# Two-layer linear attention and gated feed-forward on one core: key weights loaded as groups of full rows, first key tiles computed part by part

## The chip, the cores and the metric

One Trainium2 chip, one of its cores. The metric is the device time of one execution in microseconds (us). TensorE is called PE, VectorE DVE, ScalarE ACT, GpSimd POOL, as in the profile.

## The reference, cut to what matters

```python
def _A_ref(x, wqkv, wo):                      # linear attention, 32 heads of 32
    qkv = (x @ wqkv) ...                      # q, k, v
    phi = lambda t: jnp.where(t > 0, t + 1, jnp.exp(t)) + 1e-6
    pq, pk = phi(q), phi(k)
    kv = einsum("bhsd,bhse->bhde", pk, v); z = einsum("bhsd->bhd", pk)
    o = einsum("bhqd,bhde->bhqe", pq, kv) / (einsum("bhqd,bhd->bhq", pq, z)[..., None] + 1e-6)
    return o @ wo                             # heads merged again
def _B_ref(x, w_gate, w_up, w_down):
    return ((x @ w_gate) * (x @ w_up)) @ w_down

x = A_x                                       # 2048 tokens x 1024, bfloat16
x = x + _A_ref(_layernorm(x), A_wqkv, A_wo)
x = x + _B_ref(_layernorm(x), B_w_gate, B_w_up, B_w_down)
x = x + _A_ref(_layernorm(x), A_wqkv, A_wo)
x = x + _B_ref(_layernorm(x), B_w_gate, B_w_up, B_w_down)
```

## The kernel before

Every operation is recorded in program order for its engine; semaphore waits are derived from what it reads and writes. So the order of the calls below is the order on each engine. The change and the argument touch only the opening of the first attention layer. A token tile is 128 tokens; there are 16.

The layer norm of a tile: statistics on DVE, reciprocal root on POOL, normalisation on DVE.

```python
def ln_a(i):
    for h in range(2):   P.add("dve", bn_stats of half h of x_res[:, i])
    P.add("dve", bn_aggr)
    P.add("pool", variance + eps)
    P.add("pool", pow -0.5)                 # ln_rstd
# tiles 5, 7, 9, 11, 13: statistics by two ACT passes (ln_s1 copy with sum, ln_s2 square with sum)
# and the same POOL steps behind ln_s2; ln_b2: normalise on DVE, (x - mean) * rstd
```

A tile is then transposed, by PE and a copy out of PSUM for the first four, by DMA from tile 4 on:

```python
if self.to == "A0" and n == 0:              # tile 0 in two halves, ACT and DVE
    for hf, b in enumerate((B_TP, B_KQ[3])):
        P.add("pe", 4 transposes);  P.add(("act", "dve")[hf], copy of that half)
    return
P.add("pe", 8 transposes);  P.add("act", copy of the whole tile)
```

The opening, with `proj(kind, i, h)` the 8 matmuls of one column half of a tile and `ev` its feature map phi (exp and relu on ACT, minimum and sum on DVE):

```python
lnp.start(0); lnp.b_one(); lnp.step_t(1)    # tile 0: statistics, normalise, transpose
...three warm-up matmuls...
lnp.start(1); lnp.b_one()
# inside the first projections: transposes of tile 1 in (k,0,h=1), of tile 2 in (k,1,h=1)
mids = {("k", 0, 0): lambda: None, ("k", 0, 1): lambda: lnp.step_t(1), ("k", 1, 1): lambda: lnp.step_t(1)}
lead = [[start(2)], [b_one], [start(3)], [b_one], [], [step_t(1)], [start(4)], [b_one, start(5)]]
for kind, i in seq:                         # k0 k1 k2 q0 k3 q1 k4 ...
    for h in range(2):
        ev = proj(kind, tok[i], h, mids.pop(...)); ev()
        if lead: ...the next entry, and for k2 one weight difference (128x2048) on DVE...
        elif kind == "k": lnstep(i, h)      # h=0: start(next tile), then b_one() of the tile before
```

The loads, all on one queue:

```python
dma(x tile 0, columns 0-511); dma(x tile 0, columns 512-1023)
for hf in range(2):
    dma(k weights, rows of 4 of the 8 row blocks, columns 0-511)
xload(1); load_w("k", 1)                    # k columns 512-1023, all 8 row blocks
xload(2); load_w("q", 0); xload(3); load_w("q", 1); xload(4); xload(5)
```

## Time and profile before

| | |
|---|---|
| time, three runs at first | 1436.43 us median (1435.66 to 1438.34) |
| span of the profile | 1433.9 us |
| PE busy | 1420.6 us, 99% |
| first useful PE work | 6.46 us |
| PE restart for the second half of the key weights | 11.23 us |
| start of key tile 2 | 18.14 us |

A line of the timeline gives start, length, engine, source line, operation, output and input, shape, count, and in brackets the idle time ahead of it with what ended it. A line merges several instructions and lengths are modelled, so two lines can overlap (12.11 + 0.61 against 12.55 in the kernel before); starts are what to compare. The prediction below shows the opening's lines and reads them.

### The profile page before, as it was taken

To read this page: it belongs to the slowest core of one execution; us is meant where nothing else is said; L and a number is where in the kernel's file an instruction comes from. 1 tells how busy PE (TensorE), PEld (TensorE's weight loads), DVE (VectorE), ACT (ScalarE), POOL (GpSimd) and SP (SyncE) were. 2 spreads that over 40 slices of the span, in tenths; PEclk is the share of its full clock that TensorE was granted. 3 is DMA by queue.
4 is the path that set the end of the run, shared out by engine and by line. 5 is a ranking of instruction groups with operands and counts; after the bars stand their busy time and mean duration, and the time that the engine had idled before them with its cause. 6 is when DMAs were issued, how large, how long until landed. Compare 5 with 4: busy or idle time off the path is not lost.

```text
span 1433.9 us, 21771 instructions
## 1 busy us (share of the span) xinstructions
PE 1420.6 (99%) x8107; PEld 786.8 (55%) x8167; DVE 1209.5 (84%) x2370; ACT 688.2 (48%) x1408; POOL 149.9 (10%) x181
## 2 busy tenths in 40 slices
PE   9999999999999999999999999999999999999999
PEld 4444444555546566664544444446766475666547
DVE  6897878999988799988679978778888887888888
ACT  5882355444410266652157813667776004767400
POOL 2203621000010000002000045310000100000000
PEclk9999999999999999999999999999999999999999
DMA  7868978997786777768993266767775976777653
GB/s 227 203 144 234 219 173 199 300 303 266 255 266 211 235 256 255 244 235 300 232 286 96 89 171 165 182 181 254 262 243 194 288 256 226 261 258 259 205 192 120
DMA packets 272586, 320.73 MB, mean 224 GB/s; under 512 B 164064, under 2 KB 215008, under 8 KB 272480
## 3 DMA queue, kind: packets, MB, share of 16 engines
q1 hardware_dynamic: 272480, 319.34, 73.1%
q8 instruction: 64, 1.05, 0.3%
q14 instruction: 42, 0.34, 0.1%
HBM read 236.45 MB, written 73.40 MB: 216 GB/s over the span
## 4 chain that ended last, share of the span: by engine, by line
PE 84%; DVE 8%; ACT 2%; DMA 2%; issue 2%; POOL 1%; SPq 1%; POOLq 0%; DVEq 0%; ACTq 0%
PE ps L1385 28%; PE ps L1466 17%; PE ps L1802 14%; PE ps L1201 8%; PE ps L960 6%; PE ps L1720 5%; PE ps L1303 4%; DVE arena L798 3%; PE ps L928 2%; DMA arena<-arena 1%; DVE arena L453 1%; DVE arena L801 1%; DMA arena<-in_A_wqkv_dram 1%; ACT arena L658 1%; SPq L426 1%
## 5 line engine op out<-in xcount | busy, mean ns | idle before, releaser
L798 DVE TENSOR_TENSOR arena<-arena 128x512 f16<-128x512 f16 (+9 forms) x1019 | 498.8, 517 | 60.1 <-ACT arena L1470 34.2
L1385 PE MATMUL ps<-arena 128*128 128x512 f16 x1888 | 457.0, 379 | 1.0 <-DVE arena L801 0.9
L801 DVE SCALAR_TENSOR_TENSOR arena<-ps,arena 128x512 f16<-128x512 f32 (+3 forms) x545 | 353.8, 663 | 68.5 <-PE ps L1802 28.4
L1466 PE MATMUL ps<-arena 128*128 128x256 f16 x2184 | 287.5, 273 | 1.0 <-DVE ps L1479 1.0
L1385 PEld LDWEIGHTS ps<-arena 128*128 128x128 f16 (+1 forms) x1888 | 182.9, 98 | 163.4 <-ACT ps L1414 3.8
L1466 PEld LDWEIGHTS ps<-arena 128*128 128x128 f16 (+1 forms) x2184 | 212.2, 98 | 91.5 <-ACT arena L1470 6.9
L1802 PE MATMUL ps<-arena 128*128 128x512 bf16 (+1 forms) x1102 | 242.6, 379 | 0.9
L1802 PEld LDWEIGHTS ps<-arena 128*128 128x128 f16 x1120 | 109.5, 98 | 130.4 <-DVE arena L798 0.4
L1390 ACT ACTIVATE arena<-ps 128x512 f32<-128x512 f32 x224 | 133.8, 597 | 76.4 <-PE ps L1385 61.6
L1470 ACT ACTIVATE arena<-ps 128x256 f32<-128x256 f32 x351 | 125.1, 384 | 26.9 <-PE ps L1466 22.0
L960 PE MATMUL ps<-arena 128*128 128x512 f16 (+1 forms) x606 | 134.1, 379 | 1.0 <-ACT arena L967 0.4
L1201 PE MATMUL ps<-arena 128*128 128x512 bf16 x498 | 114.7, 379 | 0.7
L1303 PE MATMUL ps<-arena 128*128 128x512 bf16 x502 | 110.3, 379 | 0.5
L456 POOL TENSOR_SCALAR arena<-arena 128x1 f32<-128x1 f32 x59 | 20.8, 353 | 806.8 <-DVE arena L455 806.8
L1476 ACT COPY ps<-ps 128x256 f32<-128x256 f32 x182 | 66.3, 364 | 74.6 <-DVE arena L801 28.3
L960 PEld LDWEIGHTS ps<-arena 128*128 128x128 f16 x616 | 59.5, 98 | 74.7 <-ACT arena L967 5.8
L1414 ACT COPY ps<-ps 128x512 f32<-128x512 f32 x112 | 65.4, 584 | 64.3 <-PE ps L1385 52.1
L1062 POOL TENSOR_TENSOR arena<-arena 128x1024 f16<-128x1024 f32 x32 | 78.2, 2445 | 154.6 <-DVE arena L1060 146.3
L1720 PE MATMUL ps<-arena 128*128 128x256 f16 (+1 forms) x784 | 86.8, 273 | 0.7 <-DVE arena L801 0.5
L453 DVE BATCH_NORM_STATS2 arena<-arena 128x6 f32<-128x512 bf16 x118 | 81.3, 689 | 5.4 <-DMA arena<-in_A_x_dram 3.3
L1479 DVE TENSOR_TENSOR ps<-ps,arena 128x256 f32<-128x256 f32 x182 | 76.6, 427 | 10.5 <-PE ps L1466 9.5
L1303 PEld LDWEIGHTS ps<-arena 128*128 128x128 f16 x512 | 50.1, 98 | 60.4
(70 smaller groups left out, 939.8 us busy)
## 6 DMA issues: line engine op xcount, KB each, us to landing
arena<-w_scratch SPq DMA_DIRECT2D x84, 896.0 KB, 4.6
arena<-t_scratch SPq DMA_DIRECT2D x32, 896.0 KB, 6.1
arena<-in_B_w_down_dram SPq DMA_DIRECT2D x24, 896.0 KB, 5.7
arena<-sp_scratch SPq DMA_DIRECT2D x26, 768.0 KB, 4.2
w_scratch<-arena SPq DMA_DIRECT2D x28, 512.0 KB, 6.3
arena<-w_scratch SPq DMA_DIRECT2D x28, 384.0 KB, 4.8
x_scratch<-arena SPq DMA_DIRECT2D x40, 256.0 KB, 7.7
arena<-x_scratch SPq DMA_DIRECT2D x40, 256.0 KB, 5.6
```

Of the source, the lines that this page charges most:

```text
L453: P.add("dve", (lambda h: lambda e: e.bn_stats(st[j][:, 6 * h:6 * h + 6], x_res[:, i, (D // 2) * h:(D // 2) * (h + 1)]))(h), rd=r_x(i, (D ...
L798: P.add("dve", lambda e: e.tensor_tensor(out=out, in0=a, in1=b, op=op), rd=rd, wr=wr, prd=prd)
L801: P.add("dve", lambda e: e.scalar_tensor_tensor(out=out, in0=a, scalar=sc, in1=b, op0=ALU.mult, op1=op1), rd=rd, wr=wr, prd=prd)
L960: P.add("pe", lambda e: [e.matmul(psb(bank), a[0][:, k, :], b[0][:, k, :], start=(q in (1, 5) and k == 0), stop=(k == 3), skip_group_check ...
L1201: return [e.matmul(psb(bank), xrt[t][:, jj * 128:(jj + 1) * 128], pk[:, h, t, :], start=(t == tok[0]), stop=(t == tok[NST - 1])) for t in ts]
L1303: return [e.matmul(psb(bank), xnT[:, g, i * 128:(i + 1) * 128], wp[:, g, dh * 512:(dh + 1) * 512], start=(dh == 0 and g == 0), stop=(g == ...
L1385: P.add("pe", lambda e: [e.matmul(psb(bank), w[:, k, :], x[:, k, :], start=(start and k == 0), stop=(k == 3), skip_group_check=True) for k ...
L1390: P.add("act", lambda e: e.activation(t, psb(bank), AF.Copy, scale=SG), prd=[bank], wr=r)
L1466: P.add("pe", lambda e: [e.matmul(psb(bank)[:, 256 * half:256 * half + 256], w[:, k, :], xx[:, k, :], start=(start and k == 0), stop=(k == ...
L1470: P.add("act", lambda e: e.activation(d, src, AF.Copy, scale=sc), prd=[xk], wr=rd_)
L1720: P.add("pe", lambda e: [e.matmul(psb(bank)[:, 256 * half:256 * half + 256], a[:, k, 128 * r:128 * r + 128], b[:, k, :], start=(start and ...
L1802: P.add("pe", lambda e: [e.matmul(psb(bank), hv[:, 7 * hf + k, t * 128:(t + 1) * 128], w[:, k, :], start=(q in "15" and hf == 0 and k == 0 ...
```

## The change

Its intent is to have PE begin the keys as rows of the weights land, instead of waiting for whole column halves, and to get tile 1's transposes and the copies out of the way. The diff, cut to its core:

```diff
-        def ln_a(i):
+        def ln_a(i, mid=None):              # mid() is recorded between the two statistics halves
...
-                if self.to == "A0" and n == 0:
-                    for hf, b in enumerate((B_TP, B_KQ[3])):
+                if self.to == "A0" and n < 3:
+                    for hf, b in enumerate((B_TP, B_KVT[0])):
+                        dv = hf and n < 2   # tiles 0, 1: ACT and DVE; tile 2: both halves on ACT
...
-                lnp.step_t(1)
+                lnp.start(1, lambda: lnp.step_t(1))
                 ...three warm-up matmuls...
-                lnp.start(1)
...
+            if first:
+                for k in (0, 2, 4):
+                    p0(range(k, k + 2))     # column half 0 of key tile 0, two row blocks
+                    p1_(range(k, k + 2))    # column half 1
+                lnp.step_t(1)               # transposes of tile 1
+                p0(range(6, 8))
+                p1_(range(6, 8))
+                lnp.start(2)
+                lnp.b_one()
+                e0_()
+                e1_()
+                pt1(range(KT))              # key tile 1
+                pt1b(range(0, 4))
+                lnp.step_t(1)               # transposes of tile 2
+                pt1b(range(4, KT))
+                lnp.start(3)
+                et1()
+                lnp.b_one()
+                et1b()
+                seq = seq[NHOLD:]
...
-        for hf in range(2):
-            dma(wk[:, 4 * hf:4 * hf + 4, 0:512], ...)
         xload(1)
-        load_w("k", 1)
-        xload(2)
-        load_w("q", 0)
+        for k, key in ((0, KW["k"][0]), (2, KKB), (4, KW["k"][1]), (6, KKC)):
+            if k == 6:
+                xload(2)
+            w_rows("k", k, 2, key)          # two row blocks, all 1024 columns
+        w_rows("q", 0, 4, KW["q"][0])
         xload(3)
-        load_w("q", 1)
+        w_rows("q", 4, 4, KW["q"][1])
```

More of the change, by code (lines that the diff above doesn't have):

```diff
@@ L294, in build_kernel @@
     KKB = dkey("k0b")
+    KKC = dkey("k0c")
     KXS = [dkey("xs%d" % i) for i in range(NST)]
@@ L454, in ln_a @@
                       rd=r_x(i, (D // 2) * h, (D // 2) * (h + 1)), wr=R(O_ST[j] + 24 * h, 24))
+                if mid and h == 0:
+                    mid()
             P.add("dve", lambda e: e.bn_aggr(mv[j][:, 0:2], st[j]), rd=R(O_ST[j], 48), wr=R(O_MV[j], 8))
@@ L514, in dst, with start @@
                 return vh(o, D), R(o, D * 2)
-            def start(self, i):
+            def start(self, i, mid=None):
                 assert i == self.n
@@ L521, in start @@
                 else:
-                    j = ln_a(self.order[i])
+                    j = ln_a(self.order[i], mid)
                 self.n += 1
@@ L579, in transpose @@
                               rd=r + R(O_IDENT, 256), pwr=[b])
-                        P.add(("act", "dve")[hf], (lambda hf, tq_: lambda e: (e.tensor_copy if hf else e.copy)(xnT[:, 4 * hf:4 * hf + 4, i * 128:(i + 1) * 128], tq_))(hf, tq_),
+                        P.add(("act", "dve")[dv], (lambda hf, tq_, dv=dv: lambda e: (e.tensor_copy if dv else e.copy)(xnT[:, 4 * hf:4 * hf + 4, i * 128:(i + 1) * 128], tq_))(hf, tq_),
                               prd=[b], wr=_seg(O_XT + 4 * hf * S * 2, 4, S * 2, i * 256, (i + 1) * 256))
@@ L925, in proj, with ev, part @@
                 kq_i[0] += 1
+                def ev():
+                    phi_evac(bank, *dst_of(kind, i, h))
+                    if kind == "k" and tok.index(i) % 2 and h:
+                        z_pair(tok.index(i) // 2)
+                def part(ks):
+                    P.add("pe", lambda e: [e.matmul(psb(bank), xnT[:, k, i * 128:(i + 1) * 128], t[:, k, h * 512:(h + 1) * 512],
+                                                    start=(k == 0), stop=(k == KT - 1)) for k in ks],
+                          rd=r_xT(i * 128, (i + 1) * 128)[ks[0]:ks[-1] + 1] + r_w(base, h * 512, (h + 1) * 512)[ks[0]:ks[-1] + 1], pwr=[bank])
+                if mid == "parts":
+                    return part, ev
                 for ks in ((range(0, 4), range(4, 8)) if mid else (range(KT),)):
@@ L933, in proj @@
                         mid = None
-                def ev():
-                    phi_evac(bank, *dst_of(kind, i, h))
-                    if kind == "k" and tok.index(i) % 2 and h:
-                        z_pair(tok.index(i) // 2)
                 return ev
@@ L1104, in layer_A @@
             seq += [("q", i) for i in range(max(NPL - NHOLD - 1, 0), NPL if NPL < NST else 0)]
-            mids = {("k", 0, 0): lambda: None, ("k", 0, 1): lambda: lnp.step_t(1), ("k", 1, 1): lambda: lnp.step_t(1)}
-            lead = [[lambda: lnp.start(2)], [lambda: lnp.b_one()], [lambda: lnp.start(3)],
-                    [lambda: lnp.b_one()], [], [lambda: lnp.step_t(1)], [lambda: lnp.start(4)], [lambda: lnp.b_one(), lambda: lnp.start(5)]]
-            npack = [0]
+            mids = {("k", 2, 0): lambda: None}
+            lead = [[], [lambda: lnp.step_t(1)], [lambda: lnp.start(4)], [lambda: lnp.b_one(), lambda: lnp.start(5)]]
+            if first:
+                (p0, e0_), (p1_, e1_) = [proj("k", tok[0], h, "parts") for h in range(2)]
+                (pt1, et1), (pt1b, et1b) = [proj("k", tok[1], h, "parts") for h in range(2)]
+                for k in (0, 2, 4):
[17 more added lines that the diff above has]
+                seq = seq[NHOLD:]
             for kind, i in seq:
@@ L1948, in build_kernel, with w_rows @@
         dma(x_res[:, 0, dh0:D], x2[0:128, dh0:D], r_x(0, dh0, D), KXB)
-        for hf in range(2):
-            dma(wk[:, 4 * hf:4 * hf + 4, 0:512], wqkv_v[:, 4 * hf:4 * hf + 4, D:D + 512], _seg(O_WK + 8 * hf * D, 4, D * 2, 0, 1024), (KW["k"][0], KKB)[hf])
         xload(1)
-        load_w("k", 1)
-        xload(2)
-        load_w("q", 0)
+        def w_rows(n, k, m, key):
+            t, v, c0, base = WSRC[n]
+            dma(t[:, k:k + m, :], v[:, k:k + m, c0:c0 + D], R(base + k * D * 2, m * D * 2), key)
+        for k, key in ((0, KW["k"][0]), (2, KKB), (4, KW["k"][1]), (6, KKC)):
[3 more added lines that the diff above has]
+        w_rows("q", 0, 4, KW["q"][0])
         xload(3)
-        load_w("q", 1)
+        w_rows("q", 4, 4, KW["q"][1])
         xload(4)
```

## The prediction

Four passages are cut out where the marks are. The forecast's sum came to 1.7 us at key tile 2, less 0.2, so 1436.4 - 1.5 = 1434.9 us. Its 1.0 us behind the summed bytes is from the trace (10.2 to 11.19 us); that landings follow from the bytes queued ahead is my estimate, from the two landings given (tails of 1.0 and 0.85 us). The 1.014 and 0.586 us are ACT's copies of 128x1024 and of 128x512 elements out of PSUM. "The idle here" is the 1.44 us of PE ahead of 11.23; four matmuls behind it took 1.04 us, and 1.03 at 12.55. What longer idle would do is not shown. "Warm-up" is only a name for matmuls without a use for their result; no run here shows what they do for the clock.

> **What bounds the kernel now.** I read the page first, for the whole span: the share of each engine and the tenths by slice.
>
> ```profile
> span 1433.9 us, 21771 instructions
> PE 1420.6 (99%) x8107; PEld 786.8 (55%) x8167; DVE 1209.5 (84%) x2370; ACT 688.2 (48%) x1408; POOL 149.9 (10%) x181
> ...
> PE   9999999999999999999999999999999999999999
> ...
> PEclk9999999999999999999999999999999999999999
> ```
>
> TensorE (PE) is busy 99% of 1433.9 us, at the full granted clock in every slice: 13.3 us of idle in all. A change that leaves the matmul work as it is can win at most the part of that idle which it touches. This one touches the opening only, so next I read the timeline of PE in the first 25 us.
>
> ```profile
> 1.37 5.30 PE L433 MATMUL ps<-arena 128*128 128x512 f16 x12 [1.37 <-POOL arena L429]
> 6.46 0.92 PE L578 MATMUL ps<-arena 128*128 128x128 f16 x8
> 7.21 0.81 PE L1087 MATMUL ps<-arena 128*128 128x512 f16 x3
> 7.90 1.90 PE L928 MATMUL ps<-arena 128*128 128x512 bf16 x8
> 11.23 1.04 PE L928 MATMUL ps<-arena 128*128 128x512 bf16 x4 [1.44 <-DMA arena<-in_A_wqkv_dram]
> 12.11 0.61 PE L586 MATMUL ps<-arena 128*128 128x128 f16 x8
> 12.55 1.03 PE L928 MATMUL ps<-arena 128*128 128x512 bf16 x4
> 13.82 2.76 PE L928 MATMUL ps<-arena 128*128 128x512 bf16 x11 [0.24 <-ACT arena L588]
> 16.42 0.61 PE L586 MATMUL ps<-arena 128*128 128x128 f16 x8
> 16.87 1.03 PE L928 MATMUL ps<-arena 128*128 128x512 bf16 x4
> 18.14 3.63 PE L928 MATMUL ps<-arena 128*128 128x512 bf16 x16 [0.24 <-ACT arena L588]
> ```
>
> L433 and L1087 are warm-up matmuls whose result nobody uses; L578 and L586 are transposes of token tiles, L928 the key projections. So the useful work begins at 6.46 us. The first half (columns 0 to 511) of key tile 0 runs at 7.90, then PE waits until 11.23 for the second half of the key weights, then comes tile 1, with a PE pause before and behind it, where ScalarE (ACT) copies a transposed tile out of PSUM in one piece. The chain of waits of the same stretch names the same two causes.
>
> ```profile
> 3.28 7.91 DMA arena<-in_A_wqkv_dram
> ...
> 11.23 1.04 PE ps L928 x4
> 12.27 0.46 PE ps L586 x8
> ...
> 12.75 1.02 ACT arena L588
> ...
> 17.07 1.02 ACT arena L588
> ...
> 18.14 3.63 PE ps L928 x16
> ```
>
> The weight transfer lands at 3.28 + 7.91 = 11.19 us. How much is lost: a stream of 16 projection matmuls took 21.60 - 18.14 = 3.46 us, 0.216 us each; 8 transposes 0.46 us. From 7.90 to the start of key tile 2 there are 32 matmuls (6.91) and two sets of transposes (0.92), 7.83 us of work. It ends at 18.14, not 15.73: **2.4 us are lost**, 1.6 in front of 11.23 and about 0.4 at each of the two copies.
>
> Last, what follows. From 22 to 40 us the stretch view counts 83 PE matmuls; 83 times 0.216 is 17.9 of 18.0 us. PE streams without a break there although ACT (13.8 us busy) and DVE (14.9) are well loaded, so an earlier start should move everything behind it.
>
> [...] GB/s of the stretch view, summed per us, give 0.46 MB moved by 4 us, 1.12 by 6, 1.82 by 8, 2.19 by 9, 2.56 by 10, 2.92 by 11. The second key half has 2.62 MB in front of its end (tile 0 0.26, first key half 1.05, tile 1 0.26, itself 1.05), reached at 10.2 us; it landed at 11.19, a tail of 1.0 us. Tile 1 (1.57 MB, 7.3 us) released VectorE (DVE) at 8.14, a tail of 0.85.
>
> [...] I use the 1.0 us of the trace.
>
> [...] The trace has 1.014 and 0.586. So halving a copy costs ACT 0.16 us more in durations, and only two engines, or a half that overlaps other work, make it pay.
>
> [...] the idle here is 1.4 us and the matmuls behind it are at full speed, so shorter idle adds no risk.
>
> **The change, part by part.**
>
> *Order of loads.* Before: x0 (two halves), k columns 0-511 in two parts, x1, k columns 512-1023, x2, q half, x3, q half. After: x0, x1, k rows in groups 0, 1, 2 (0.52 MB each, 2 KB runs instead of 1 KB), x2, group 3, then q as two groups of rows with x3 between. Landings by the curve above plus 1.0 us: group 0 ends at 1.05 MB, 5.8 + 1.0 = 6.8 us; group 1 at 1.57 MB, 8.3; group 2 at 2.10 MB, 9.7; group 3, behind x2, at 2.88 MB, 11.9. The full runs may help: once only x tiles (2 KB runs) were left in the queue, after 18 us, the rate was 377 to 391 GB/s, against about 355 while 1 KB runs were in it. At 384 GB/s from 4 us on, group 3 ends 6.3 us later, 10.3, and lands at 11.3. I take 11.6, group 2 at 9.5, group 1 at 8.1.
>
> *Token tile 1 earlier.* It lands near 5 us and no longer holds DVE. Its first statistics half (0.7 us) runs while PE transposes tile 0, at 6.25; the copy of tile 0's second half stays at 7.4 to 7.8, since the transposes release it; then the second statistics half to 8.55, and by the spacing of before (bn end 9.56 to normalised 11.36, 1.8 us) tile 1 is ready at 10.35 instead of 11.36.
>
> *Parts by rows.* PE: 4 matmuls (both halves, two rows) are 0.86 us. Group 0 from 7.9 to 8.77; group 1 is there, to 9.63; group 2 (9.5), to 10.5; transposes of tile 1 to 10.95, in what was idle; wait for group 3 until 11.6; its 4 matmuls to 12.46. The only loss left is 0.65 us.
>
> *Copies in halves.* Tile 1's halves go to ACT and DVE side by side and are done by 11.7, before PE comes to it at 12.46: the first 0.4 us pause goes. Tile 1 takes 12 matmuls (2.59) to 15.05, tile 2's transposes to 15.5, 4 matmuls to 16.36. Tile 2's halves are both on ACT, the first as soon as four transposes are out, 15.3, the second 0.5 later and done near 16.37. Key tile 2 starts near 16.42: the second pause is 0.06 us. Tile 2's normalisation has to be ready by 15.05: statistics from 11.6 (behind the DVE copy), 1.42 + 1.8, gives 14.85. It just is.
>
> *Sum.* 18.14 - 16.42 = **1.7 us earlier**; 1.4 if group 3 lands at 11.9, 1.9 if at 11.3, where tile 2's normalisation begins to bind. No matmul, transpose or byte is added or removed; ACT has one copy instruction more, DVE one more; PE is cut into one group more.
>
> *Farther on.* q tile 0 now needs all q rows: 2.88 + 2.36 = 5.24 MB, some 18.5 us with the tail, and PE comes to it at about 20.5. Hidden. ACT holds the four exp/relu pairs of tiles 0 and 1 closer together (14.5 to 19 us without a break), but PSUM banks are asked for again only from 20 us. I take off 0.2 us for small losses: **1.5 us** at the end, 1436.4 - 1.5 = **1434.9 us**, 0.1%.
>
> **The rivals.**
>
> 1. *The last weight group becomes the wait.* x1 and x2 both go ahead of it, 0.26 MB more than before the old second half, 0.7 us at the measured rate. For: the queue is full from 4 us on (DMA share 0.94 or more). Against: only 4 matmuls wait for it, not 24. If the full rows bring nothing and the mixed issue order costs something, group 3 lands at 12.5 and the gain is 0.8 us: 1435.6.
>
> 2. *The gain is given back in the next stage.* The chain of waits from 26 to 60 us runs through ACT, DVE and POOL, and PE pauses 0.43 us for ACT near 39.5, so PE has little lead over them there. If those engines, not PE, set the pace of 20 to 60 us, and the bunched exp/relu work puts them behind, the time stays at 1436.4. Against: they were waiting for PE themselves at 22 to 24 us (ACT 0.64 and 0.18 us), so they move with it.
>
> 3. *Tile 2 late.* DVE has to wait out tile 2's POOL steps before it finishes tile 0's keys; if statistics start later than 11.6, PE waits in front of tile 2's transposes, up to some 0.5 us: 1435.4.
>
> 4. *Everything fits and the loads are faster*: at most the 2.4 us lost, 1434.0.
>
> **Range and chances.** Rivals and landing times spread the gain over 0 to 2.2 us. The three times of before span 1435.7 to 1438.3, so the median of a few runs is itself uncertain by about 1 us, and other timings of later transfers can move either way by as much. Together I put 8 in 10 on 1433.2 to 1436.9. A change of 2% is 29 us, over ten times what the opening holds, and twice all of PE's idle; nothing in it can cost as much either. Faster 0.005, same 0.99, slower 0.005.
>
> **What would show it right or wrong.** In the changed profile: key matmuls begin near 7.9 in pieces of 4; the wait for weights shrinks from 1.4 to about 0.65 us and ends near 11.6; transposes of tile 1 stand before that wait; no PE pause of 0.4 us in front of tile 1; key tile 2 starts near 16.4 instead of 18.14; the PE pause of 39.5 us moves to about 38, no longer than before. I am wrong if group 3 lands after 12.5, if PE waits in front of tile 2's transposes, or if the lead at 16.4 is gone at 40 or 60 us.

## The result, and the profile after

The changed kernel: 1434.53 us median (1433.85 to 1434.79, 4 runs); the kernel before in the same rounds 1436.05 us (1435.22 to 1438.34, 4 runs). The ratio is 0.9986 with a 95% interval of 0.9969 to 1.0003. Ratios here are the mean time of one kernel's runs over that of the other's of the same rounds, so not quite the ratio of the medians quoted.

The page of the changed kernel, the lines that answer to the first fence of the prediction:

```profile
span 1432.5 us, 21777 instructions
PE 1420.4 (99%) x8107; PEld 786.5 (55%) x8167; DVE 1210.1 (84%) x2371; ACT 687.8 (48%) x1409; POOL 148.5 (10%) x181
```

PE's busy time is the same within 0.2 us; the span is 1.4 us shorter. So idle went, as forecast. The PE timeline of the changed kernel's opening (L937 and L943 are key projections here, L582 transposes):

```profile
7.65 2.75 PE L937 MATMUL ps<-arena 128*128 128x512 bf16 x12
10.24 0.61 PE L582 MATMUL ps<-arena 128*128 128x128 f16 x8
11.09 3.63 PE L937 MATMUL ps<-arena 128*128 128x512 bf16 x15 [0.23 <-DMA arena<-in_A_wqkv_dram]
14.55 0.61 PE L582 MATMUL ps<-arena 128*128 128x128 f16 x8
15.00 1.03 PE L937 MATMUL ps<-arena 128*128 128x512 bf16 x4
16.11 3.63 PE L943 MATMUL ps<-arena 128*128 128x512 bf16 x16
```

Twelve key matmuls run without a break from 7.65 (three groups of rows had landed in time), tile 1's transposes follow, and the wait for the last group is 0.23 us where it was 1.44. Key tile 2 starts at 16.11 instead of 18.14: a lead of 2.03 us, more than the 1.7 forecast. But the PE timeline of the same kernel goes on like this:

```profile
31.12 7.08 PE L943 MATMUL ps<-arena 128*128 128x512 bf16 x31 [0.58 <-DMA arena<-arena]
38.93 6.43 PE L943 MATMUL ps<-arena 128*128 128x512 bf16 x28 [0.73 <-ACT arena L662]
```

against, in the kernel before:

```profile
39.91 5.35 PE L928 MATMUL ps<-arena 128*128 128x512 bf16 x24 [0.43 <-ACT arena L658]
```

PE now waits at 31 us for tile 4, which a transposing DMA brings ("arena<-arena"), and its pause near 39 us is longer. Of the 2.03 us it has 0.98 left. Following the matching lines farther: 0.96 at the first product of the Strassen-like part (68.29 against 67.33), 1.49 at 249 us (249.50 against 248.01), 1.4 at the end. Two questions follow: what takes half of the lead back, and how firm any of these numbers is.

### The profile page after: what moved, and what is told of

Read it like the earlier page. It is cut to its first block, busy times and chain, and to the rows that moved or that the text cites. A ratio compares the mean times of both kernels' runs of the same rounds, so it can differ in the third digit from the quotient of the medians.

```text
span 1432.5 us, 21777 instructions
## 1 busy us (share of the span) xinstructions
PE 1420.4 (99%) x8107; PEld 786.5 (55%) x8167; DVE 1210.1 (84%) x2371; ACT 687.8 (48%) x1409; POOL 148.5 (10%) x181
## 3 DMA queue, kind: packets, MB, share of 16 engines
q8 instruction: 64, 1.05, 0.3%
## 4 chain that ended last, share of the span: by engine, by line
PE 86%; DVE 8%; ACT 2%; issue 2%; DMA 1%; POOL 1%; SPq 0%; POOLq 0%; DVEq 0%
PE ps L1414 28%; PE ps L1495 17%; PE ps L1831 14%; PE ps L1230 8%; PE ps L1332 6%; PE ps L970 6%; PE ps L1749 5%; DVE arena L802 4%; DVE arena L454 1%; PE ps L943 1%; DVE arena L805 1%; DMA arena<-arena 1%; DVE arena L649 1%; ACT arena L662 1%; PE ps L1256 1%
```

## The experiments

The theory at the start (A): the opening's gain comes from the row groups with parts, not from halved copies; half of it is given back since tile 4's normalisation on DVE, behind two weight differences, came only 1.0 us earlier while PE came 2.0 us earlier. The rival (R1): PE's pace alone decides, and differences later are chance. A second rival (R2): ACT's bunched exp and relu work holds PE back.

Landmarks from all profiles, in us, are collected here; the text refers to them. "Last weight part" is PE's restart for the last part of the key weights, "statistics of tile 6" is the start of that DVE instruction, "after 39" PE's restart from the pause near 39 us, "quads" the first product of the part that follows the plain projections.

| kernel | last weight part | key tile 2 | statistics of tile 6 | after 39 | difference | quads | at 249 | span |
|---|---|---|---|---|---|---|---|---|
| before | 11.23 | 18.14 | 30.50 | 39.91 | 9.41 | 68.29 | 249.50 | 1433.9 |
| before_again | 11.03 | 17.93 | 30.30 | 39.69 | 9.39 | 68.08 | 249.11 | 1433.8 |
| changed | 11.09 | 16.11 | 29.53 | 38.93 | 9.40 | 67.33 | 248.01 | 1432.5 |
| changed_again | 12.18 | 17.20 | 30.39 | 39.80 | 9.41 | 68.19 | 248.97 | 1433.1 |
| whole_copies | 12.06 | 17.24 | 29.72 | 39.11 | 9.39 | 67.48 | 247.59 | 1431.5 |
| short_runs | 12.13 | 17.46 | 30.50 | 39.89 | 9.39 | 68.26 | 249.28 | 1433.1 |
| dummy5 | 11.46 | 17.31 | 29.66 | 39.06 | 9.40 | 67.43 | 248.86 | 1432.9 |
| early_tile4 | 11.79 | 16.80 | 29.96 | 39.36 | 9.40 | 67.72 | 248.46 | 1432.5 |
| no_parts | 11.13 | 18.74 | 31.22 | 40.62 | 9.40 | 68.99 | 249.85 | 1433.9 |
| swap_first | 11.65 | 16.67 | 31.14 | no pause | | 66.46 | 247.15 | 1431.3 |
| swap_first_early4 | 11.86 | 16.88 | 31.06 | no pause | | 66.36 | 247.47 | 1431.5 |
| swap_whole | 12.09 | 17.27 | 31.03 | no pause | | 66.33 | 246.79 | 1430.7 |
| before_swap | 11.08 | 17.98 | 31.63 | no pause | | 66.93 | 248.51 | 1435.0 |

### whole_copies: the halved copies of tiles 1 and 2 undone

```diff
-                if self.to == "A0" and n < 3:
+                if self.to == "A0" and n < 1:
```

> The changed kernel with the transposed tiles 1 and 2 copied whole on ScalarE again. If halving the copies is what removed the two 0.4 us pauses, both come back: key tile 2 starts near 16.9 us instead of 16.1. My theory: tile 1's pause went because its transposes now stand ahead of the last weight part, so a whole copy (1.02 us) still fits in there; only tile 2 loses 0.1 to 0.2 us: start at 16.2 to 16.3. Time within 0.3 us of the changed kernel either way, since PE waits again at 31 us.

Correct; 1434.33 us median (1433.25 to 1434.95, 4 runs), before 1437.03, ratio 0.9983 (0.9968 to 0.9998). Its PE timeline:

```profile
12.06 3.63 PE L937 MATMUL ps<-arena 128*128 128x512 bf16 x16 [0.47 <-DMA arena<-in_A_wqkv_dram]
15.52 0.61 PE L590 MATMUL ps<-arena 128*128 128x128 f16 x8
15.97 1.03 PE L937 MATMUL ps<-arena 128*128 128x512 bf16 x4
17.24 3.63 PE L943 MATMUL ps<-arena 128*128 128x512 bf16 x16 [0.24 <-ACT arena L592]
```

The weights landed 1 us later in this run than in the first profile, so only distances can be compared. From the last part to key tile 2 it takes 5.18 us, and 5.02 in the changed kernel in both its profiles (11.09 to 16.11, 12.18 to 17.20). Whole copies thus cost 0.16 us, all of it in front of tile 2, and 16 matmuls run from 12.06 without a pause ahead of tile 1. Halving the copies did not remove the pause ahead of tile 1; the earlier place of its transposes did.

They also hold DVE up further on. In the changed kernel DVE cannot start tile 2's statistics before its half of tile 1's copy, and that waits for PE. The table shows it: with landings 0.12 us apart (12.06, and 12.18 in changed_again), tile 6's statistics start at 29.72 without that copy and at 30.39 with it.

### short_runs: the same groups in 1 KB runs

```diff
-            w_rows("k", k, 2, key)
+            for hf in range(2):
+                dma(t[:, k:k + 2, hf * 512:(hf + 1) * 512], ..., (key, KKH[k // 2])[hf])
```

> Row groups in the same order, but each of the four as two transfers of column halves, so runs of 1 KB instead of 2 KB. If the run length sets the rate: 355 to 365 GB/s instead of 383 to 408 between 5 and 12 us, PE restarts for the last weight part at 11.7 to 12.0 instead of 11.1, key tile 2 starts at 16.7 to 17.0. If the faster queue comes from the order of the loads alone: rate and starts as in the changed kernel.

Correct; 1434.68 us (1434.62 to 1435.06, 4 runs), ratio 0.9984 (0.9971 to 0.9998). In the stretch view it moves 378 and 372 GB/s from 8 to 10 and 10 to 12 us; the changed kernel 396 and 385 in one profile, 373 and 405 in the other, and the kernel before 372 and 360. So the longer runs moved some 4% more here taken together (a mean of 390 GB/s against 375), less than the 8% I had read off the queue's end. The larger gap exists, though: from 12 to 18 us, where mostly q weights move, the same view has 351 to 359 GB/s in the kernel before (q in 1 KB runs) and 385 to 390 in the changed kernel (q in 2 KB runs), 9% in the means. Length and order of the q loads changed together there, so no run says which of the two it is. The restart at 12.13 us lies within what unaltered loads give (11.09 to 12.18), so the share of the run length in the landing time is not settled by this run.

### dummy5: 1.08 us of useless work put on PE on purpose

```diff
                 et1b()
+                P.add("pe", 5 matmuls of zeros into a free bank)
```

> Five unused matmuls of 0.216 us (1.08 us) on PE ahead of key tile 2, nothing else. My theory, that about half of the 2.0 us lead is given back at 31 and 39 us because tile 4's normalisation on VectorE came only 1.0 us earlier: key tile 2 starts at 17.2 us, the wait for tile 4's transposing DMA at 31 us vanishes, PE is where the changed kernel is by 40 us, and the time is the same within 0.2 us. Rival, PE alone sets the pace: everything behind is 1.1 us later, 1435.6.

Correct; 1434.74 us (1433.96 to 1434.93, 4 runs), ratio 0.9983 (0.997 to 0.9997). Its PE timeline, around the inserted matmuls and near 39 us:

```profile
16.23 1.24 PE L1137 MATMUL ps<-arena 128*128 128x512 f16 x5
17.31 3.62 PE L943 MATMUL ps<-arena 128*128 128x512 bf16 x16
...
39.06 6.22 PE L943 MATMUL ps<-arena 128*128 128x512 bf16 x28 [0.42 <-ACT arena L662]
```

Key tile 2 starts 1.20 us later than in the first profile of the changed kernel (0.37 by the later landing, 0.83 by the inserted work, since 0.25 us of its 1.08 fell into the pause that stood there); 22 us on, PE is 0.13 us behind, the wait at 31 us is gone, the pause near 39 is 0.42 instead of 0.73, and the time is the same within 0.2 us. A delay of PE of 1.2 us is free. R1 falls: between 20 and 39 us something other than PE sets the end.

### early_tile4: tile 4's statistics ahead of the weight differences

```diff
-            lead = [[], [step_t(1)], [start(4)], [b_one, start(5)]]
+            lead = [[start(4)], [step_t(1), b_one], [], [start(5)]]
```

> The changed kernel with tile 4's statistics ahead of the first weight difference on VectorE and its normalisation ahead of the second. My theory: PE no longer waits for tile 4's transposing DMA near 31 us (0.6 to 0.7 us less), the pause of 0.73 us at 38.9 shrinks too, since ScalarE waits there behind tile 4 by way of POOL; PE at 60 us is 0.7 to 1.1 us earlier and the time 0.5 to 1.0 us less, near 1433.7. Rival, the bunched exp and relu work of ScalarE is what holds PE: both pauses stay and the time is 1434.5.

Correct; 1434.66 us (1434.21 to 1436.19, 5 runs), ratio 0.9987 (0.9974 to 0.9999). PE near 39 us:

```profile
39.36 6.00 PE L943 MATMUL ps<-arena 128*128 128x512 bf16 x27 [1.22 <-ACT arena L662]
```

The wait near 31 us is gone, as theory A had it. But the pause near 39 grew from 0.73 to 1.22 us and nothing was won. Theory A named a real wait, not the one that binds: what PE no longer lost at 31 it lost at 39. The table's column of differences says what does bind. In all nine profiles where PE pauses near 39 us (three of them taken later), it restarts 9.39 to 9.41 us after DVE starts tile 6's statistics, with leads of PE that differ by 2.6 us. So I looked at what lies between the two. POOL and DVE of the changed kernel there:

```profile
31.27 0.21 POOL L459 TENSOR_SCALAR arena<-arena 128x1 f32<-128x1 f32 x1 [3.42 <-DVE arena L458]
31.57 0.57 POOL L465 TENSOR_TENSOR arena<-arena 128x1 f32<-128x1 f32 x1
32.20 0.19 POOL L480 TENSOR_SCALAR arena<-arena 128x1 f32<-128x1 f32 x1
32.48 0.56 POOL L465 TENSOR_TENSOR arena<-arena 128x1 f32<-128x1 f32 x1
```

```profile
29.53 1.42 DVE L454 BATCH_NORM_STATS2 arena<-arena 128x6 f32<-128x512 bf16 x2
30.98 0.21 DVE L458 BATCH_NORM_AGGREGATE arena<-arena 128x2 f32<-128x12 f32 x1
33.07 0.55 DVE L495 TENSOR_SCALAR arena<-arena 128x1024 f16<-128x1024 bf16 x1 [1.88 <-POOL arena L465]
```

The first two POOL lines are tile 6's, the next two tile 5's. Tile 5's sum of squares was ready on ACT at 29.1 us, but POOL comes to it only at 32.20: tile 6 stands ahead of it in the order of the calls, and for that POOL sits idle for 3.42 us, until DVE's statistics are there. DVE, whose next call is tile 5's normalisation, then stands 1.88 us for it. ACT waits behind DVE (2.75 us, until 34.31) for a relu buffer, and PE behind ACT. The new theory (B): this knot, entered when DVE reaches tile 6, sets PE's time after 39 us; its entry time, not PE's, carries any gain.

### changed_again: the changed kernel once more

No edit.

> The changed kernel itself, unaltered, to see how much of its opening repeats. In the four runs before this one, with the same loads up to the last weight group, PE restarted at 11.46 to 12.13 us instead of 11.09. If landing times scatter: restart between 11.0 and 12.1 and key tile 2 between 16.1 and 17.2, but PE at its pause near 39 us within 0.4 us of 38.93, and the wait of VectorE for a transposing DMA near 224 us anywhere from 2.0 to 3.2 us. If the variants caused it: 11.1 and 16.1 again. Time 1434.5 within 0.5.

Correct; 1435.04 us (1434.09 to 1436.03, 5 runs), before 1437.06, ratio 0.9988 (0.9976 to 1.0001). Its PE timeline:

```profile
10.25 1.02 PE L937 MATMUL ps<-arena 128*128 128x512 bf16 x4 [0.41 <-DMA arena<-in_A_wqkv_dram]
...
12.18 3.63 PE L937 MATMUL ps<-arena 128*128 128x512 bf16 x15 [0.46 <-DMA arena<-in_A_wqkv_dram]
...
17.20 3.63 PE L943 MATMUL ps<-arena 128*128 128x512 bf16 x16
```

The landing of the last group scatters between profiles of identical loads: 11.09 and 12.18 us here, 11.46 to 12.09 in the variants that keep these loads and parts. From 4 to 6 us these loads moved 271 to 352 GB/s. PE's restarts for the last two groups are 1.93 to 1.96 us apart in every profile with unaltered loads and parts that paused ahead of both (in early_tile4 and swap_first_early4 the trace puts the first of the two down to DVE), which is 0.79 MB at 405 GB/s; the scatter arises earlier. From 4 to 8 us the queue moved 1.50 MB in the first profile and 1.30 in this one (352 against 297 GB/s from 4 to 6 us, 398 against 351 from 6 to 8). At 400 GB/s, near the 405 above, that is an estimated 0.5 us of the 1.09; where the rest comes from is not shown. I expected PE within 0.4 us of 38.93 near 39 us; it was at 39.80. That fits B, since DVE entered tile 6 at 30.39, and speaks against an entry time that doesn't depend on the weights. It does, by the route found in whole_copies: group 2 lands, PE transposes tile 1, DVE copies its half (10.89 us in the first profile, 11.76 here, 11.03 in dummy5) and from there to tile 6 runs for 18.63 to 18.64 us in all three. In this stretch the timeline names only waits of DVE for POOL (1.00, 0.46 and 0.46 us), none for ACT. In the kernel before, DVE waited six times for ACT between 12 and 26 us, 2.43 us in all, and ACT for PE (1.00 us at 15.76, ahead of the second line). Three lines of its DVE:

```profile
14.30 0.29 DVE L645 TENSOR_SCALAR arena<-arena 128x512 bf16<-128x512 bf16 x1 [0.71 <-ACT arena L649]
...
16.39 0.29 DVE L645 TENSOR_SCALAR arena<-arena 128x512 bf16<-128x512 bf16 x1 [0.65 <-ACT arena L649]
...
30.50 1.42 DVE L453 BATCH_NORM_STATS2 arena<-arena 128x6 f32<-128x512 bf16 x2
```

So DVE followed PE there before the change; in the changed kernel it runs at its own pace.

### swap_first: tile 5 normalised ahead of tile 6's statistics

```diff
                 if h == 0:
+                    if first and i == 3:
+                        lnp.b_one()
                     if lnp.n < NST:
                         lnp.start(lnp.n)
-                    lnp.b_one()
+                    if not (first and i == 3):
+                        lnp.b_one()
```

> The changed kernel with one pair of steps exchanged: tile 5 is normalised before tile 6's statistics start, so that tile 5's reciprocal root no longer stands on POOL behind tile 6's. New theory of the give-back: this order stalls VectorE 1.9 us near 31 us and ScalarE 2.75 us behind it, and the pause of PE at 39 us is its end. Then the VectorE stall falls to about 0.5 us, the pause of 0.73 us at 39 goes, PE at 60 us is 0.6 to 0.8 earlier and the time 1433.8. If the wait for tile 4's transposing DMA is what counts: the pause stays and the time is 1434.5.

Correct; 1433.3 us (1433.06 to 1435.22, 5 runs), before 1437.06, ratio 0.9979 (0.9966 to 0.9991). DVE there:

```profile
30.68 0.55 DVE L495 TENSOR_SCALAR arena<-arena 128x1024 f16<-128x1024 bf16 x1 [0.74 <-POOL arena L465]
31.14 1.42 DVE L454 BATCH_NORM_STATS2 arena<-arena 128x6 f32<-128x512 bf16 x2
```

DVE's stall fell from 1.88 to 0.74 us, PE's pause near 39 us is gone, and PE reaches the quads at 66.46: 0.87 us earlier than in the changed kernel's first profile although its key tile 2 started 0.56 later, and 1.73 earlier than in its second. That the knot holds PE near 39 us is confirmed by undoing it alone. R2 falls as the cause of this pause, since ACT's exp and relu work is the same. Two waits of PE are left, 0.33 us for tile 4 at 31 us and 0.32 us for ACT near 63.

### swap_first_early4: both edits

> Both edits: tile 4 earlier and tile 5 ahead of tile 6. By the new theory neither the wait near 31 us nor the pause near 39 us is left, the whole lead of the opening (1.3 to 2.0 us by when the weights land) is still there at 60 us, and the time is 1433.2 to 1433.8. If ScalarE's load itself is the limit: a pause of 0.4 us or more stays before 45 us and the time is 1434 or more.

Correct; 1433.44 us (1432.8 to 1435.84, 5 runs), ratio 0.9979 (0.9966 to 0.9993). PE has no wait between key tile 2 and 62.9 us, so up to there the lead of the opening is fully kept; then comes one pause of 0.37 us. From key tile 2 to the quads it takes 49.48 us (16.88 to 66.36). Over swap_first alone it wins 0.3 us of PE waiting and nothing that the times resolve.

### no_parts: the row groups without the parts

```diff
-                for k in (0, 2, 4):
-                    p0(range(k, k + 2))
-                    p1_(range(k, k + 2))
                 lnp.step_t(1)
-                p0(range(6, 8))
-                p1_(range(6, 8))
+                p0(range(KT))
+                p1_(range(KT))
```

> The changed kernel with the two halves of key tile 0 each computed in one piece of 8 matmuls, loads as they are; so PE waits for all four groups before its first key matmul. If computing part by part is what makes the row groups pay: first key matmul at 11.1 to 12.1 us, key tile 2 at 18.2 to 19.2, no earlier than in the kernel before, yet at 39 us PE is at most 1 us behind the changed kernel since PE has slack there; time 1434.7 to 1435.8. If row groups pay by themselves (longer runs): key tile 2 near 16.5 to 17.

Correct; 1438.83 us (1435.92 to 1439.29, 4 runs), before 1437.06, ratio 1.001 (0.9996 to 1.0023).

```profile
9.84 0.62 PE L582 MATMUL ps<-arena 128*128 128x128 f16 x8 [2.26 <-DVE arena L495]
11.13 6.22 PE L937 MATMUL ps<-arena 128*128 128x512 bf16 x27 [0.67 <-DMA arena<-in_A_wqkv_dram]
...
18.74 1.47 PE L943 MATMUL ps<-arena 128*128 128x512 bf16 x6
```

PE idles from 7.6 to 9.84, waits again to 11.13, and key tile 2 starts at 18.74, 0.6 to 0.8 us later than before the change. Loading full rows pays only with the parts. After 39 us PE is 1.69 us behind the changed kernel's first profile, more than the 1.0 I allowed, 0.82 behind the second. The median is 3 us more than I expected, but it rests on the three runs at 1438.48 to 1439.29, whose granted clock was 0.997 to 0.999. The one run at 1.0, which was profiled, took 1435.92; the six runs at 1.0 of the kernel before in these rounds have a median of 1436.59. So the extra 3 us go with the lower clock. Why the clock was lower is not shown.

### before_again and before_swap

before_again is the kernel before with no edit; before_swap has the exchange of swap_first alone.

> The kernel before, unaltered, as a second sample of its opening and as a check of the ratio (1.000). Theory from the eight profiles so far: PE restarts after its pause near 39 us 9.40 us behind the start of tile 6's statistics on VectorE, whatever PE's own lead. So restart minus that start is 9.3 to 9.5 us here too. If the weight landings scatter as in the changed kernel, the restart for the second key half lies between 11.0 and 12.5 us (11.23 in the first profile) and key tile 2 between 17.9 and 19.4.

Correct; 1435.58 us (1435.0 to 1436.74, 5 runs) against 1436.5 of the same kernel in the same rounds (9 runs), ratio 0.9995 (0.9982 to 1.0007). So medians of identical kernels can differ by 0.9 us (0.6 if the three of the nine runs with a clock of 0.999 are left out); smaller differences of medians here carry nothing. The restart came at 11.03 us, at 11.08 in before_swap: the old loads scatter less than the new ones (11.03 to 11.23 against 11.09 to 12.18). The difference to tile 6's statistics is 9.39.

> The kernel before with tile 5 normalised ahead of tile 6's statistics, nothing else. If the tied chain of VectorE, POOL and ScalarE binds PE at 39 us only by what PE leads it, the kernel before gains just its pause of 0.4 us: time 0.2 to 0.6 us less than the kernel before, and the change plus the exchange stays 2 to 3 us ahead of this. If the exchange is worth its 1.7 us by itself, 1.5 us or more.

Correct; 1434.77 us (1434.43 to 1436.79, 5 runs), before 1436.5, ratio 0.9988 (0.9974 to 1.0001). I expected 0.2 to 0.6 us. The medians say 0.8 against before_again and 1.7 against the nine other runs, too little and too uneven to settle it; the profile does:

```profile
21.89 45.20 PE L928 MATMUL ps<-arena 128*128 128x512 bf16 x208
66.93 3.40 PE L960 MATMUL ps<-arena 128*128 128x512 bf16 x14
```

From key tile 2 to the quads PE takes 48.95 us, and 50.15 in both profiles of the kernel before, as the pause of 0.36 us near 64 us went along with that of 0.4 near 39. So the knot was there before the change too (DVE stands the same 1.88 us at 34.05), and cost it 1.2 us. The exchange is thus worth about the same on both kernels: the changed kernel takes 51.22 and 50.99 us over this way, swap_first 49.79. With the exchange on both sides the lead still falls, from 1.31 us at key tile 2 (17.98 against 16.67) to 0.47 at the quads (66.93 against 66.46), by the two waits that swap_first has left. The knot explains where PE restarts near 39 us; it is not the only thing that takes a lead back. (The profiled run was this kernel's slowest, 1436.79; past 249 us it took 1186.5 us, all others 1183.8 to 1184.7.)

### swap_whole: the version that the runs point to

The changed kernel with whole copies for tiles 1 and 2 and the exchange; both edits as above.

> The changed kernel with tiles 1 and 2 copied whole on ScalarE and tile 5 normalised ahead of tile 6. VectorE then does not wait for tile 1's transposes in the opening. No pause of PE near 39 us, and none near 31; PE at 60 us is set by when the weights landed: the gap between the start of key tile 2 and the first quad product is 49.2 to 49.5 us of work without pauses but for 0.36 at 63 us. Time 1433.0 to 1434.0, within 0.5 us of the exchange alone.

Correct; 1432.54 us (1432.51 to 1433.13, 5 runs), before 1436.5, ratio 0.9974 (0.9961 to 0.9986). PE from key tile 2's end on:

```profile
21.18 45.31 PE L943 MATMUL ps<-arena 128*128 128x512 bf16 x208
66.33 3.84 PE L970 MATMUL ps<-arena 128*128 128x512 bf16 x16
```

208 matmuls of 0.216 us are 44.9 us: PE streams without a single pause from 21 to 66 us, and takes 49.06 us from key tile 2 to the quads. I had expected 49.2 to 49.5 with a pause of 0.36, and 1433.0 to 1434.0. Of the lead over before_swap, 0.71 us at key tile 2 (its weights landed late), 0.60 is left at the quads. It is the fastest of all kernels by median: 4.0 us under the nine runs of the kernel before, 3.6 under the six of them at clock 1.0, 3.0 under before_again, 2.2 under before_swap, all in the same rounds; and 2.0 to 2.5 us under the two medians of the changed kernel, though it was not timed in the same rounds as that.

## Why the prediction was right or wrong

The time forecast, 1434.9 us, was met: 1434.53, and 1435.04 in the second call. Its parts were less right than its sum, and the last point shows that the sum was met with the help of something that the prediction did not contain. Unless the change itself shortens that wait, which is open, that was luck.

- **PE as the bound, and the size of the stakes.** Right: busy time unchanged, only idle moved, 0.1%.
- **Landings by summed bytes.** Group 3 was put at 11.6 us, 11.3 to 11.9. The profile of the changed kernel has 11.09, the eight profiles with these loads and parts 11.09 to 12.18, mean 11.8. On average this holds; the scatter of 1.1 us was not foreseen, and is nearly as large as the gain itself. The tail behind the summed bytes, taken as 1.0 us, comes out at 0.95 us in the first profile (2.88 MB moved by 10.14 us, restart at 11.09); for the other seven I estimate 1.1 to 1.45 us from their rates of 4 to 12 us, with the first profile's 0.54 MB moved by 4 us taken for all. The first profile was the earliest of them: in the other seven PE also waits 0.15 to 0.41 us ahead of group 2's matmuls (for DMA in five, put down to DVE in two), which the prediction had in time.
- **Parts by rows.** Right, and needed: without them the new loads put key tile 2 at 18.74.
- **Tile 1 earlier.** Right: normalised at 10.03 (forecast 10.35), its transposes fill PE's idle time ahead of the last part.
- **Copies in halves.** Wrong. Both pauses of 0.4 us were booked to the halving. The one ahead of tile 1 went by the new order. The one ahead of key tile 2 was put at 0.06 us and is 0.25 (four matmuls from 15.00, 0.86 us, then nothing until 16.11); with whole copies it is 0.41. DVE's share of tile 1's copy also ties its later work to PE: tile 6's statistics came 0.67 us later with it, 0.12 of that by the landing.
- **Key tile 2 at 16.42.** 16.11 and 17.20; the mean lead over the two profiles of each kernel is 18.04 - 16.66 = 1.4 us, against 1.7.
- **"I take off 0.2 us for small losses."** This is the step that failed. Between key tile 2 and the restart near 39 us the lead fell from 2.03 to 0.98 us in the first profiles, from 1.4 to 0.44 in the mean of two each. It is the second rival, in a form that the prediction did not see: not ACT's bunched work, but DVE's own pace, with POOL's order of tiles 5 and 6 behind it. The prediction argued from ACT's waits at 22 to 24 us that ACT, DVE and POOL wait for PE and so move with it. ACT did (the pair that starts at 21.80 us before starts at 19.77 after, behind a wait of 0.64 us for PE in both). DVE no longer waited for ACT after the change (no such wait from 10.89 to 29.53 us), and came to tile 6 only 0.44 us earlier (29.96 against 30.40 in the mean); 9.40 us behind it PE restarts. The pause near 39 us, said to be no longer than before, grew from 0.43 to 0.73. A wrong reading helped to hide it: PE does not stream "without a break" from 22 to 40 us; the view that counts 83 matmuls has it busy for 17.46 of the 18.00 us.
- **Why the sum was still met.** Taking both profiles of each kernel, the mean lead is 1.4 us at key tile 2, 0.4 at the quads, 0.8 at 249 us and 1.05 in the span; the times say 1.5 and 2.0. The increase from the quads to 249 us lies in a wait of PE for DVE at 244 us: 0.93 and 0.74 us before, 0.39 and 0.38 after. DVE stands behind a transposing DMA near 224 us, for 3.22 and 3.03 us before, 2.69 and 2.67 after, 2.04 to 3.12 in the variants of the changed kernel, and 3.59 in before_swap. Whether the change shortens that wait or the samples happened to fall so is open, and so is the last half microsecond between spans and times, which is below what identical kernels differ by.

## What to carry to other kernels

A lead won on the busiest engine is worth what the engines tied to it can follow (here 0.98 of 2.03 us past 39 us): look for the next pause of that engine and ask when the work that ends it was started, not only who ended it. POOL served the tiles in the order of its calls: tile 5's step, ready at 29.1 us, ran at 32.20, behind tile 6's. So where one helper engine serves several tiles, the tile whose input is ready first should be issued first; here that took DVE's stall from 1.88 to 0.74 us. Before crediting one part of a change, undo that part alone: here the halved copies got credit that belonged to the order of the transposes. And try a repair on the kernel before as well: the exchange, found as the cure of a loss, was worth 1.2 us there too.
